# Third copy buffers, moved layernorm statistics, a later store in the output projection and an early exponential, in a fused attention and gated-MLP kernel

## Chip, core and metric

The kernel runs on one core of one Trainium2 chip. The metric is the device time of one execution in microseconds (us). The time before is the median of three runs. Engines are named as in the profile: PE (TensorE, matmuls and transposes; PEld is its weight load), DVE (VectorE), ACT (ScalarE), POOL (GpSimd), SP (SyncE, which issues the DMAs here; SPq is its queue).

## What is computed

```python
def _A_ref(x, wqkv, wo):                      # x: 1 x 2048 x 576
    H = 32; Dh = D // H; W = 256              # Dh = 18
    q, k, v = heads of x @ wqkv
    scores = q @ k.T * Dh ** -0.5
    mask = (i - j >= 0) & (i - j < W)
    p = softmax(where(mask, scores, -1e9))
    return (p @ v) @ wo

def _B_ref(x, w_in, w_sp, b_sp, w_out):       # w_in: 576 x 4608, w_sp: 2048 x 2048
    z = gelu(x @ w_in)
    z1 = z[..., :Fh];  z2 = layernorm(z[..., Fh:])
    g = w_sp @ z2 + b_sp                      # over the tokens
    return (z1 * g) @ w_out

xn = layernorm(x)
out = x + _A_ref(xn) * silu(_B_ref(xn))
```

## The kernel before

Every fp32 product is made of three products of rounded halves: a value's high part is rounded by ACT, its low part is the DVE's difference of the value and the high part (`split`, L115 and L116). PE therefore has most of the work. One execution goes through these stages, one after the other on PE.

**Stage 1, 0 to 57 us.** x comes in four chunks of 512 tokens. For each chunk DVE makes the layernorm statistics (`stats_of`, L303 and L304: four tiles with two BN_STATS and a BN_AGGR each), and a chain of one square root on ACT (L119) and seven small DVE instructions makes scale and shift (`scales_of`, L120 to L125 and L310). ACT normalizes (`norm_act`, L327), PE transposes eight 64-column blocks and then a ninth (`turn_group`, L337, PSUM tile `tpt`), and `form` splits the result: ACT the high part (L352), DVE the low part (L354). In between PE makes the first products for q and k, `narrow(j, c)` (L380): five column groups j of the weights for the 256 tokens of c, 54 matmuls each into a pair of PSUM banks, `ma` and `mb`. `keep_narrow` empties the pair into `qkhl`, ACT the high half (L115), DVE the low half (L116). All queues run in program order, so the place of `stats_of(2)` and `scales_of(2)` in the text is their place in DVE's queue.

**57 to 428.6 us.** The rest of q and k, v (copied out of PSUM at L909), and z2 with its Gelu on ACT (L946).

**Attention with z1 as filler, 428.6 to 894.4 us.** Sixteen units: eight groups of four heads for each half of the tokens. Each unit needs, in this order:

- *maxima*: matmuls `sp` (L598), whose row maximum DVE takes (L602, tile `mx`); `max_split` makes `ms` (L612); when all 32 are there, `max_end` transposes `ms` on PE (L621), DVE copies it (`mhl`, L624) and four DMAs write it as two extra rows into `att`, the tile that holds q (L628). These rows are what subtracts the maximum in the scores;
- *scores*: matmuls `tps` (L722), exponential on ACT (`pt`, L726), triangle masks on POOL (L734, L737);
- *pv*: products of `pt` with v into one PSUM bank `ops` (L750, one buffer), copied by ACT into `ou` (L765) when four blocks of rows are done;
- *the end of a unit* (`finish`): the sums of the exponentials are one row per head of `ou`; they go by DMA to `den`, are inverted by DVE (`invert`, L785), go to DRAM and come back spread over the partitions in `rp` (L792); POOL multiplies in four pieces (`divide`, L796) and four DMAs store the result (L801, o_d).

The maxima, the scores and the 1944 matmuls of z1 (`ma`, `mb`, L669, copied by ACT into `z1o` at L674 and stored at L571) each use half of PE's rows, so that two *lanes* run side by side; pv products and the transpose use all of its rows and both lanes stand still for them. The order is found while the program is built: a planner keeps a clock for each lane and for the busy time of the other engines, and in a loop takes whatever its rules allow: `pv_now` and `pv_run` for pv, `max_end` for full maxima, then the scores and maxima, and a fill matmul when nothing else is ready. A list `waiting` holds what is to be issued at a later reading of the planner's clock (loads, the steps of `finish` at `INVERT_AT`, `FETCH_AT` and `DIVIDE_AT`). The planner's clock decides the order alone; it is no time of the chip.

**wo, 894.4 to about 955 us.** Sixteen blocks n of 28 matmuls each (L1155) multiply the attention result by wo; `wo_load(t)` fetches what blocks 2t and 2t+1 need, `wo_split(t)` splits it (`ohl`, L1141 and L1142). The last unit is finished inside this loop: its sums are fetched at n == 1, divided and stored at n == 2. Each block's result is copied by ACT (`so`, L1188) and stored one block later (s_d, L1190).

**955 us to the end.** The product with w_sp (L1434), then with w_out (L1525), sum and store.

## Time and profile before

| | before |
|---|---|
| three runs | 1858.68, 1856.02, 1855.85 us |
| median | 1856.02 us |
| profiled execution | 1856.53 us, of which 1854.5 us are the span of the trace |
| attention stage | 465.8 us, of which PE is busy 452.22 us |
| wo stage, 894.4 to 955 us | 60.6 us, PE busy 60.18 us |
| TensorE clock over the execution | 0.995 of full speed |

The span goes from the first to the last instruction of the trace; 2.03 us of the profiled execution lie around it. Rows that group instructions read: line, engine, operation, output <- inputs, shapes, count, busy us, mean ns, and idle time of the engine just ahead of them, with what ended it. Rows of the timeline read: start, duration, engine, line, and in brackets the idle time before. A row of waits gives the engine and the line that waited, what it waited for, the total in us, how often, and the longest.

### The profile page before, as it was taken

Reading aid. Unit: us, or ns where it says so; the run is one execution under the profiler, and the core shown is the slowest. Engines: PE = TensorE matmul, PEld = TensorE weight load, DVE = VectorE, ACT = ScalarE, POOL = GpSimd, SP = SyncE. Lnnn points to the kernel's source line nnn. Section 1 sums busy time; section 2 is a strip of 40 time slices with the busy share of each in tenths; the row PEclk is TensorE's granted clock in tenths of the full one; section 3 lists DMA queues with packets and bytes.
Section 4 is the critical chain, followed back from the end, with each engine's and each line's share of the span. In section 5 each row is a group of like instructions: output and inputs, shape, how many; then the busy total and the mean of one; then the engine's idle time right before and its main releaser. Section 6 shows DMA issues by size and latency. Waiting matters only on the chain.

```text
span 1854.5 us, 38148 instructions
## 1 busy us (share of the span) xinstructions
PE 1821.4 (98%) x14357; PEld 1588.3 (86%) x14357; DVE 1138.4 (61%) x2283; ACT 948.4 (51%) x1756; POOL 432.0 (23%) x507
## 2 busy tenths in 40 slices
PE   8999999998999999999999999999999999999998
PEld 7999999997777777776898878888888888899998
DVE  6411333456776767771246787667976576767876
ACT  5533322224666567667467565465454544444443
POOL 3332333334455455555100000021200000000000
PEclk8999999999999999999999999999999999999999
DMA  8795688887566666755777677788777556797554
GB/s 265 189 231 172 226 278 284 288 261 215 144 185 173 194 180 178 195 161 147 232 259 247 220 242 244 262 281 296 257 259 246 181 194 210 222 263 217 160 160 134
DMA packets 266920, 405.75 MB, mean 219 GB/s; under 512 B 52336, under 2 KB 180592, under 8 KB 266608
## 3 DMA queue, kind: packets, MB, share of 16 engines
q1 hardware_dynamic: 266736, 403.32, 70.8%
q8 instruction: 113, 1.85, 0.4%
q14 instruction: 71, 0.58, 0.1%
HBM read 285.35 MB, written 117.09 MB: 217 GB/s over the span
## 4 chain that ended last, share of the span: by engine, by line
PE 84%; DVE 6%; DMA 5%; SPq 2%; ACT 2%; issue 2%; POOL 0%; DVEq 0%; ACTq 0%; POOLq 0%
PE acc L1434 35%; PE mb L206 12%; PE c L1525 8%; PE ma L669 6%; PE mb L669 5%; PE ops L750 4%; PE ma L206 4%; PE tps L722 3%; PE sp L598 2%; PE wops L1155 2%; SPq L363 1%; DMA xr<-in_x_dram 1%; PE ma L380 1%; DMA st_d<-qkhl 1%; DVE junk L602 1%
## 5 line engine op out<-in xcount | busy, mean ns | idle before, releaser
L1434 PE MATMUL acc<-spl,zh 128*128 128x512 f32 x1008 | 392.7, 390 | 1.3 <-DVE spl L116 1.2
L1434 PE MATMUL acc<-sph,zl 128*128 128x512 f32 x1008 | 392.2, 389 | 0.0
L1434 PE MATMUL acc<-sph,zh 128*128 128x512 f32 x1008 | 392.1, 389 | 0.0
L602 DVE CUSTOM_DVE_ANT_0 junk<-sp,band 128x384 bf16<-128x384 f32 (+1 forms) x512 | 275.8, 539 | 114.1 <-PE sp L598 32.7
L726 ACT ACTIVATE pt<-tps 128x384 f32<-128x384 f32 (+2 forms) x576 | 232.0, 442 | 121.1 <-PE tps L722 77.9
L116 DVE TENSOR_TENSOR spl<-spr,sph 128x1024 fp32r<-128x1024 f32 x168 | 209.7, 1248 | 38.7 <-ACT sph L115 37.8
L669 PE MATMUL mb<-b,z1wh 64*128 64x512 f32 x648 | 225.8, 401 | 2.2 <-ACT z1o L674 1.7
L669 PE MATMUL ma<-b,z1wh 64*128 64x512 f32 x648 | 225.0, 399 | 0.6 <-ACT zt L946 0.4
L1434 PEld LDWEIGHTS acc<-spl,zh 128*128 128x128 f32 x1008 | 189.2, 188 | 42.4 <-DVE spl L116 3.3
L1434 PEld LDWEIGHTS acc<-sph,zh 128*128 128x128 f32 x1008 | 189.2, 188 | 39.3
L1434 PEld LDWEIGHTS acc<-sph,zl 128*128 128x128 f32 x1008 | 189.2, 188 | 39.2
L115 ACT ACTIVATE zh<-b 128x384 fp32r<-128x384 f32 x168 | 87.6, 521 | 213.6 <-PE acc L1434 213.5
L115 ACT ACTIVATE sph<-spr 128x1024 fp32r<-128x1024 f32 x168 | 176.1, 1048 | 12.4 <-DMA spr<-sc_d 7.2
L722 PE MATMUL tps<-att 56*128 56x384 f32 (+1 forms) x576 | 177.6, 347 | 3.9 <-DMA att<-mhl 2.6
L116 DVE TENSOR_TENSOR zl<-b,zh 128x384 fp32r<-128x384 f32 x168 | 98.4, 586 | 124.1 <-ACT zh L115 121.6
L598 PE MATMUL sp<-att 54*128 54x384 f32 (+1 forms) x512 | 161.6, 350 | 1.6 <-DVE mx L602 1.4
L1525 PE MATMUL c<-b,o 128*128 128x288 f32 x1056 | 143.9, 295 | 1.5 <-DVE o L116 1.4
L1525 PEld LDWEIGHTS c<-b,o 128*128 128x128 f32 x1056 | 141.0, 188 | 2.4 <-DVE o L116 2.2
L947 DVE BATCH_NORM_STATS2 st<-zt 128x6 f32<-128x384 f32 x96 | 49.2, 547 | 131.4 <-ACT zt L946 131.3
L669 PE MATMUL ma<-b,z1wl 64*128 64x512 f32 x324 | 128.9, 398 | 0.0
L669 PE MATMUL mb<-b,z1wl 64*128 64x512 f32 x324 | 128.5, 397 | 0.0
L722 PEld LDWEIGHTS tps<-att 56*128 56x128 f32 x576 | 100.3, 185 | 32.6 <-issue 9.5
(220 smaller groups left out, 4187.6 us busy)
## 6 DMA issues: line engine op xcount, KB each, us to landing
spr<-sc_d SPq DMA_DIRECT2D x96, 512.0 KB
spr<-in_w_sp_dram SPq DMA_DIRECT2D x72, 512.0 KB
zr<-z_d SPq DMA_DIRECT2D x144, 192.0 KB
z_d<-zt SPq DMA_DIRECT2D x48, 384.0 KB
z_d<-z1o SPq DMA_DIRECT2D x72, 256.0 KB
z1t<-z_d SPq DMA_DIRECT2D x72, 256.0 KB
y_d<-z1t SPq DMA_DIRECT2D x72, 256.0 KB
a<-in_w_sp_dram SPq DMA_DIRECT2D x64, 256.0 KB
```

The lines of the kernel that those rows point to most:

```text
L115: act.activation(hi, src, AF.Copy)
L116: dve.tensor_tensor(lo, src, f32(hi), ALU.subtract)
L206: pe.matmul(banks[h][:, :n], *both[h][i], start=i == 0, stop=i == STEPS - 1)
L598: pe.matmul(ps[:, :w], q_of(u, j)[0:54, i * P:(i + 1) * P], k_of(u, j)[0:54, k0:k0 + w], start=True, stop=True)
L602: dve.tensor_tensor_reduce(out=junk[:, :w], in0=ps[:, :w], in1=band[:, m0:m0 + w], scale=1.0, scalar=-3.0e38, op0=ALU.add, op1=ALU.max, ac ...
L669: pe.matmul(ps, w, x_, start=n == 0, stop=n == STEPS - 1)
L722: pe.matmul(ps[:, :m * P], k_of(u, j)[:, (kb - base) * P:(kb - base + 1) * P], q_of(u, j)[:, (a - lo) * P:(a - lo + m) * P], start=True, s ...
L726: act.activation(pt[:, j, d0:d0 + n * P], ps[:, (qa - a) * P:(qa - a + n) * P], AF.Exp, scale=scale)
L750: pe.matmul(o_ps[c][32 * j:32 * j + 32, (qa - 4 * c) * P:(hi - 4 * c + 1) * P], vgs[u][:, kb - k0, j * VW:j * VW + 32], pt[:, j, (qa - kb) ...
L947: dve.bn_stats(st2[:, s, pc, :], zv)
L1434: pe.matmul(acc[j], z[:, ps], w[:, cs], start=s == i == 0 and n in OPENS, stop=s == 7 and i == 2, skip_group_check=True)
L1525: pe.matmul(banks[key][:, :288], y, w, start=begin and k == n == 0, stop=close and k == 8 and n == 2, skip_group_check=True)
```

## The change

- **Attention, buffers:** three `ou` tiles instead of two, two `rp` instead of one, three `z1o` instead of two. With them the steps of a unit's end come later: inversion, fetch and division have new planner times, and leftover parts are forced out three units behind instead of two (`part(u - 3)`), or when more than four are left two units behind.
- **Attention, planner:** pv is not begun while the copy out of the only `ops` bank is still under way (`ops_free`), and a run of pv products ends after a copy. The transpose of the maxima waits 1000 ns of the planner's clock after `ms`, and is taken on its own only when one of the next eight scores belongs to its unit. The first unit's scores are held 2500 ns longer. What is due is issued in the order of its due time.
- **Stage 1:** `stats_of(2)` moves from behind `keep_narrow(2, 0)` to behind `keep_narrow(4, 0)`, and `scales_of(2)` from ahead of `narrow(4, 0)` to behind `keep_narrow(0, 1)`.
- **Exponential:** one exponential of one column stands in the text ahead of the attention loop.
- **wo:** the last unit's sums are fetched after the store of block 0's result instead of before; the division stays at n == 2; its four stores move from n == 2 to n == 4, where the loads for t = 4 and t = 5 now both stand.

Every engine issues the same instructions as before, by kind and number, apart from the one exponential and one more table load on ACT.

```diff
-INVERT_AT = 6500
-FETCH_AT = 8500
-DIVIDE_AT = (20000, 21200, 22400, 23600, 26500, 27000, 27500, 28000)
+INVERT_AT = 11000
+FETCH_AT = 8000
+DIVIDE_AT = (28000, 29200, 30400, 31600, 37000, 38000, 39000, 40000)
+LATE = 1000
+DUE = 8
...
             keep_narrow(2, 0, banks)
-            stats_of(2, range(4))
             wq_high(4)
...
             form(*forms)
-            scales_of(2, range(4))
             banks = narrow(4, 0)
             form(turn_group(1, [8]))
             fetch(6, w_qk[6])
             keep_narrow(4, 0, banks)
+            stats_of(2, range(4))
             for j in range(5):
                 banks = narrow(j, 1)
...
                 keep_narrow(j, 1, banks)
                 done = None
+                if j == 0:
+                    scales_of(2, range(4))
                 if j < 2:
                     norm_act(2, (2 * j, 2 * j + 1))
                 if j == 0:
                     stats_of(3, range(4))
...
-                for w in list(waiting):
+                for w in sorted(waiting, key=lambda w: w[0]):
...
-                max_ready[u] = clock + wait + 400 + MAX_NS
+                max_ready[u] = clock + wait + 400 + MAX_NS + (2500 if u == 0 else 0)
...
-                                zo = zw.tile([P, 512], F32, name="z1o", bufs=2)
+                                zo = zw.tile([P, 512], F32, name="z1o", bufs=3)
...
+            ops_free = [0.0]
...
-                        while parts.get(u - 2):
-                            part(u - 2)
-                        ous[u] = (ap_.tile([P, HS], F32, name="ou", bufs=2) if u < NU - 1 else
+                        while parts.get(u - 3):
+                            part(u - 3)
+                        ous[u] = (ap_.tile([P, HS], F32, name="ou", bufs=3) if u < NU - 1 else
                                   tail()[:, 0:HS])
...
                     free_at = use("act", 500, 120)
+                    ops_free[0] = free_at
...
+                while len(parts.get(u - 2, ())) > 4:
+                    part(u - 2)
-                rp = ap_.tile([P, HS], F32, name="rp", bufs=1) if u < NU - 1 else f32(slots[4][:, 0:HS])
+                rp = ap_.tile([P, HS], F32, name="rp", bufs=2) if u < NU - 1 else f32(slots[4][:, 0:HS])
...
-                    after(max(INVERT_AT - sooner, 4500), invert)
+                    after(4500 if sooner else INVERT_AT, invert)
...
-                        after(ns - sooner + (3500 if sooner else 0), partial(part, u))
+                        after(ns - (14500 if sooner else 0), partial(part, u))
...
                 load_v(0)
+                warm = aa.tile([P, 1], F32, name="warm", bufs=1)
+                act.activation(warm, eps_t, AF.Exp)
...
+                def max_due(v):
+                    queue = score_queue[0]
+                    return not queue or queue[min(DUE, len(queue) - 1)][0] >= v
+
                 def pv_now():
+                    if not o_ps and ops_free[0] + GUARD > clock:
+                        return 0
...
-                    for v in [v for v in maxima if taken.get(v) == 2 * RMN and max_done[v] <= clock]:
+                    for v in [v for v in maxima if taken.get(v) == 2 * RMN and max_done[v] + LATE <= clock]:
...
                             later.clear()
                             break
+                        if not o_ps:
+                            break
...
-                    full = [v for v in maxima if taken.get(v) == 2 * RMN and max_done[v] + GUARD <= clock]
+                    full = [v for v in maxima if taken.get(v) == 2 * RMN and max_done[v] + LATE <= clock
+                            and max_due(v)]
...
                 if n == 0:
                     put_last()
-                if n == 1:
-                    sums()
                 if n == 2:
                     divide()
+                if n == 4:
                     store()
-                if n in (0, 2, 4, 6, 8):
+                    oraws.append(wo_load(4))
+                if n in (0, 4, 6, 8):
                     oraws.append(wo_load(3 + n // 2))
...
                 if stores:
                     sp.dma_start(*stores.pop())
+                if n == 1:
+                    sums()
                 stores.append((s_d[n * P:(n + 1) * P, :], so))
```

**DVE in stage 1.** Before, in DVE's queue behind `keep_narrow(2, 0)`; `st_533` are the statistics of chunk 2, the rows L354 are the low parts of chunk 1's transposes:

```order
L116 TENSOR_TENSOR qkhl<-mb,qkhl 128x256
L303 BN_STATS st_533<-xr 128x6 x2
L304 BN_AGGR st_534<-st_533 128x2
L303 BN_STATS st_533<-xr 128x6 x2
L304 BN_AGGR st_534<-st_533 128x2
L303 BN_STATS st_533<-xr 128x6 x2
L304 BN_AGGR st_534<-st_533 128x2
L303 BN_STATS st_533<-xr 128x6 x2
L304 BN_AGGR st_534<-st_533 128x2
L116 TENSOR_TENSOR qkhl<-ma,qkhl 128x256
L116 TENSOR_TENSOR qkhl<-mb,qkhl 128x256
L354 TENSOR_TENSOR b_95<-tpt,b_92 128x256
```

Now, further on in the same queue, from the last of chunk 2's statistics (`st_732`) to the first of chunk 3's (`st_826`); ahead of these rows the low parts L356 follow the two `qkhl` pairs directly:

```order
L305 BN_STATS st_732<-xr 128x6 x2
L306 BN_AGGR st_733<-st_732 128x2
L118 TENSOR_TENSOR qkhl<-ma,qkhl 128x256
L118 TENSOR_TENSOR qkhl<-mb,qkhl 128x256
L122 RECIPROCAL st_736<-st_734 128x4
L123 TENSOR_SCALAR st_735<-st_733 128x4
L124 TENSOR_TENSOR st_735<-st_735,st_736 128x4
L125 TENSOR_TENSOR st_735<-st_735,st_736 128x4
L126 TENSOR_SCALAR st_735<-st_735 128x4
L127 TENSOR_TENSOR st_736<-st_736,st_735 128x4
L312 SCALAR_TENSOR_TENSOR st_735<-st_733,st_736 128x4
L305 BN_STATS st_826<-xr 128x6 x2
```

The `qkhl` pair in the second list empties `narrow(0, 1)`. Behind it stand chunk 2's chain and all of chunk 3's statistics, and only then the pair that empties `narrow(1, 1)`; chunk 2's statistics stand right ahead of it instead of ahead of chunk 1's low parts.

**PE at a change of the `ops` bank.** Before, in a later unit of attention. The first row merges two pv products for four heads each: the last four matmuls of one bank's content and the first four of the next.

```order
L722 MATMUL tps<-att_2214 128x384
L669 MATMUL mb<-b_97,z1wh 128x512
L669 MATMUL ma<-b_97,z1wh 128x512
L722 MATMUL tps<-att_2213 128x384
L750 MATMUL ops<-pt,vg 32x128 x8
L750 MATMUL ops<-pt,vg 32x256 x4
L722 MATMUL tps<-att_2213 128x384
```

Now, at such a change in the same stage:

```order
L754 MATMUL ops<-pt,vg 32x256 x4
L754 MATMUL ops<-pt,vg 32x128 x4
L601 MATMUL sp<-att_2215 128x384
L726 MATMUL tps<-att_6835 128x256
L726 MATMUL tps<-att_6837 128x256
L601 MATMUL sp<-att_6833 128x384
L601 MATMUL sp<-att_2215 128x384
L672 MATMUL ma<-b_93,z1wh 128x512
L672 MATMUL mb<-b_96,z1wh 128x512
L672 MATMUL ma<-b_96,z1wh 128x512
L672 MATMUL mb<-b_93,z1wl 128x512
L754 MATMUL ops<-pt,vg 32x128 x4
```

Before, a row with `32x128 x8` stands at four places, and none is left; between the last product of one bank and the first of the next there are now always scores, maxima or fill matmuls.

**ACT around the exponentials.** Before, from the end of z2 to the first scores:

```order
L946 ACTIVATE zt<-mb 128x384
L119 ACT_TABLE_LOAD
L119 ACTIVATE sd_6816<-mv_84,eps_t 128x16
L674 ACTIVATE z1o<-mb 128x512
L674 ACTIVATE z1o<-ma 128x512
L684 ACTIVATE z1wh<-z1raw 128x384 x3
L726 ACT_TABLE_LOAD
L726 ACTIVATE pt<-tps 128x384 x7
```

Now, first where the new exponential stands (`qkhl` are the last of q and k, `ve` the copies of v), then at the first scores:

```order
L287 ACTIVATE wv1h<-wraw 128x9x96
L117 ACTIVATE qkhl<-ma 128x512
L117 ACTIVATE qkhl<-mb 128x512
L1016 ACT_TABLE_LOAD
L1016 ACTIVATE warm<-eps_t 128x1
L916 ACTIVATE ve<-ma 128x16x18
L916 ACTIVATE ve<-mb 128x16x18
```

```order
L953 ACTIVATE zt<-mb 128x384
L121 ACT_TABLE_LOAD
L121 ACTIVATE sd_6816<-mv_84,eps_t 128x16
L677 ACTIVATE z1o<-mb 128x512
L677 ACTIVATE z1o<-ma 128x512
L687 ACTIVATE z1wh<-z1raw 128x384 x3
L677 ACTIVATE z1o<-mb 128x512
L677 ACTIVATE z1o<-ma 128x512
L730 ACT_TABLE_LOAD
L730 ACTIVATE pt<-tps 128x384 x18
```

The new exponential, with a table load of its own, has gone ahead of the copies of v, far in front of z2's Gelu and the square root, and the load ahead of the first `pt` is still there.

6 lines of the change are left out of this document (3 added, 3 removed).

## The prediction

> **What bounds the kernel now.** I begin with the page: the busy shares, then the granted clock in 40 slices.
>
> ```profile
> span 1854.5 us, 38148 instructions
> PE 1821.4 (98%) x14357; PEld 1588.3 (86%) x14357; DVE 1138.4 (61%) x2283; ACT 948.4 (51%) x1756; POOL 432.0 (23%) x507
> PEclk8999999999999999999999999999999999999999
> ```
>
> PE is busy for 1821.4 of 1854.5 us, so 33.1 us of idle time is all that an order of work can win, and beside it what a halved clock costs. No instruction but one exponential and its table load is added or taken away, so every term below is a wait or a stretch at a lower clock. The second view is the busy time by stage (columns: PE, PEld, DVE, ACT, POOL, then clock, DMA share, GB/s).
>
> ```profile
> 0.00:57.00 57.00, 48.45 (x700) 46.61 (x702) 37.39 (x124) 33.08 (x68) 23.49 (x18) 0.91 0.80 258
> 428.60:894.40 465.80, 452.22 (x4425) 344.30 (x4426) 294.29 (x1043) 304.50 (x742) 243.11 (x355) 0.99 0.64 176
> 894.40:955.00 60.60, 60.18 (x450) 59.90 (x451) 16.11 (x19) 30.32 (x44) 3.53 (x2) 1.00 0.75 246
> ```
>
> The change touches these three stages. PE is idle for 8.55 us of the first, 13.58 us of attention and 0.42 us of wo. The third view says what PE waited for, over the whole span; the fourth groups PE's pv products, POOL's division and ACT's copy in attention.
>
> ```profile
> PE sp L621 <- DVE ms L612: 2.9, 5, 0.9
> PE tpt L337 <- DVE b L354: 2.9, 1, 2.9
> PE tps L722 <- DMA att<-mhl: 2.6, 1, 2.6
> PE mb L669 <- ACT z1o L674: 1.7, 4, 0.9
> PE wops L1155 <- DVE ohl L1142: 0.4, 1, 0.4
> ```
>
> ```profile
> L750 PE MATMUL ops<-pt,vg 128*32 128x128 f32 x448 | 23.5, 281 | 4.3 <-ACT ou L765 1.9 <-issue 1.7 <-POOL ou L796 0.8
> L796 POOL TENSOR_TENSOR ou<-ou,rp 128x256 f32<-128x256 f32 x60 | 43.6, 745 | 16.0 <-DMA rp<-r_d 14.1 <-DMA att<-st_d 1.9
> L765 ACT ACTIVATE ou<-ops 128x512 f32<-128x512 f32 x30 | 18.1, 604 | 10.9 <-PE ops L750 9.6 <-DMA o_d<-ou 1.2
> ```
>
> These are the waits that the parts of the change name: the transpose for `ms`, the low parts of stage 1, the first unit's rows, the fill for `z1o`, wo for `ohl`, and pv for the copy out of its bank.
>
> **The change part by part**, against the profiled execution of 1856.53 us (its span of 1854.5 and 2.03 around it; the runs' median, 1856.02, is 0.5 lower).
>
> *The first unit's scores.* The timeline shows the wait, and slices of 3.41 us show the clock around it (the column ahead of the last two is the clock).
>
> ```profile
> 444.30 0.45 PE L722 MATMUL tps<-att 56*128 56x384 f32 x2 [2.65 <-DMA att<-mhl]
> 441.90:445.30 3.40, 1.00 (x10) 1.00 (x11) 0.42 (x3) 0.78 (x2) 2.45 (x3) 1.00 0.56 152
> 445.30:448.72 3.42, 2.85 (x16) 2.14 (x14) 1.25 (x5) 2.62 (x5) 0.32 (x1) 0.51 0.86 251
> 448.72:452.13 3.41, 3.41 (x21) 3.12 (x18) 1.54 (x8) 1.69 (x4) 0.90 (x2) 0.50 0.70 169
> ```
>
> PE stood for 2.65 us, and in the two slices behind it 2.85 + 3.41 = 6.26 us of work ran at half clock, which is 3.1 us lost. Now the pace of a fill matmul in one lane, from the end of the stage:
>
> ```profile
> 893.00 0.40 PE L669 MATMUL ma<-b,z1wh 64*128 64x512 f32 x1
> 893.24 0.39 PE L669 MATMUL ma<-b,z1wl 64*128 64x512 f32 x1
> ```
>
> It is 0.24 us, and by width 0.18 us for 384 columns. Between unit 0's transpose and its first score there stood 42 fill and 10 maximum matmuls; by the order it is 60 and 13. Shared by two lanes that is 18 x 0.24 / 2 + 3 x 0.18 / 2 = 2.4 us more. So 0.25 us of the wait is left and the clock stays: **-5.5** (2.4 + 3.1). If the rows land 2 us later than before as well, nothing is won: bounds -5.7 and 0.
>
> *The ops bank.* 4.3 us of PE idle ahead of pv in the grouped row. All four merged `32x128 x8` rows are gone and other work stands there. At the fifth wait ACT's copy itself waited 1.2 us for the stores of an older `ou` (the L765 row), which the third buffer removes. I take four fifths, since the copy's 0.6 us is hidden only where enough matmuls follow: **-3.5** (bounds -4.3 and -1).
>
> *The transposes.* 2.9 us in five waits. They now come 1000 ns of the planner's clock later, or join a pv run; again four fifths: **-2.3** (bounds -2.9 and 0).
>
> *Third z1o.* The fill's waits of 1.7 us on ACT have one cause that a buffer can remove, this one:
>
> ```profile
> 644.61 0.60 ACT L674 ACTIVATE z1o<-mb 128x512 f32<-128x512 f32 x1 [0.96 <-DMA z_d<-z1o]
> ```
>
> **-1.0** (bounds -1.0 and 0).
>
> *The lanes.* The planner's new order also balances the lanes anew. Between two steps that need all of PE's rows, the stretch lasts as long as the longer lane. Counting each lane's matmuls in each stretch of the order and pricing them at 0.24 us for 512 columns and less by width, the longer lanes sum to 319 us before and 322 us now; 83 stretches with pv or a transpose behind them in both: **+2.7** (bounds 0, if a lane that is ahead only meets an engine later, and +2.7).
>
> *wo.* The 0.4 us wait for `ohl` has a visible chain.
>
> ```profile
> 914.74 0.65 ACT L1188 ACTIVATE so<-wops 128x576 f32<-128x576 f32 x1 [7.74 <-DMA s_d<-so]
> 902.96 3.53 POOL L796 TENSOR_TENSOR att<-att,att 128x512 f32<-128x512 f32 x2 [15.74 <-DMA att<-r_d]
> ```
>
> SP stood at the four stores until POOL's division ended at 906.5; the s_d stores behind it were late, so ACT stood for 7.74 us, and the next `ohl` with it. Behind the moved stores now stand the loads for t = 4 and 5, whose data block 8 needs; wo's 60.6 us hold 16 blocks, 3.8 us each, so from n == 4 there are 15 us, and the division has 7.6 us more before SP meets its stores: **-0.4** (bounds -0.4 and 0).
>
> *Statistics.* a row of ACT's and five of DVE's timeline in stage 1, and then PE by slices, the last three rows for the matmuls of `narrow` alone:
>
> ```profile
> 29.78 0.39 ACT L115 ACTIVATE qkhl<-mb 128x256 fp32r<-128x256 f32 x1
> 29.00 0.81 DVE L303 BATCH_NORM_STATS2 st<-xr 128x6 f32<-128x288 f32 x2
> 32.74 0.41 DVE L116 TENSOR_TENSOR qkhl<-ma,qkhl 128x256 fp32r<-128x256 f32 x1
> 33.41 3.38 DVE L354 TENSOR_TENSOR b<-tpt,b 128x256 fp32r<-128x256 f32 x8
> 36.70 0.17 DVE L120 RECIPROCAL st<-st 128x4 f32<-128x4 f32 x1
> 37.84 0.42 DVE L354 TENSOR_TENSOR b<-tpt,b 128x256 fp32r<-128x256 f32 x1
> ```
>
> ```profile
> 32.30:35.70 3.40, 1.44 (x23) 1.00 0.89 259
> 36.79:42.64 5.85, 5.84 (x54) 5.85 (x56) 0.51 1.00 300
> 42.64:45.71 3.07, 3.07 (x58) 3.07 (x56) 1.00 1.01 395
> 48.77:51.83 3.06, 3.06 (x58) 3.04 (x54) 1.00 0.61 139
> ```
>
> Before, the statistics held DVE from 29.00 to 32.74, 3.75 us, then came the low parts; PE's ninth transposes waited 2.9 us for them, the slice from 32.30 held 1.96 us of idle, and `narrow(0, 1)` ran at half clock, 5.85 instead of 3.07 us. Without the statistics DVE's `qkhl` pair follows ACT's, which ends at 30.17, and the low parts start at about 30.65, 2.75 us earlier; the wait goes, and PE starts `narrow(0, 1)` at 36.79 - 2.75 = 34.05 at full clock; after it `narrow(1, 1)` and `narrow(2, 1)` end at 43.25. But `narrow(3, 1)` needs the banks of `narrow(1, 1)`, and DVE comes to them late: low parts to 34.05, the ninth (0.42) and `qkhl(4, 0)` (0.75), with ACT's parts ahead of them, to 35.9, chunk 2's statistics to 39.65, `qkhl(0, 1)` at 0.75 to 40.4, the chain (36.70 to 37.84, 1.14) to 41.5, chunk 3's statistics to 45.25, `qkhl(1, 1)` to 46.0. So what is late next is DVE, and PE waits 2 to 2.7 us there, say 2.4, until 45.65. Before, `narrow(3, 1)` began at 48.77: 3.1 us won, if the clock stays up. Where PE stood for 2.40 of 3.40 us (441.90) and for 1.96 (32.30), the next slice was granted half. A wait of 2.4 us is as long, so I take one slice at half clock, 1.7 us: **-1.4** (bounds -3.1 at full clock and +0.3 with two slices at half).
>
> [...]
>
> *The early exponential.*
>
> ```profile
> 444.81 1.28 ACT L726 ACT_TABLE_LOAD   x1 [2.62 <-issue]
> 144.44 0.41 ACT L909 ACTIVATE ve<-ma 128x288 f32<-128x288 f32 x1 [1.33 <-POOL ve L908]
> ```
>
> It stands ahead of the copies of v now, where ACT was idle for 1.33 us waiting for POOL: that hides its load of 1.28 us. The load ahead of the first `pt` stays, so nothing is won: **0** (bounds -1.3 if the load at 444.81 were off the path after all, +1.3 if the new one is on it).
>
> *Sum*: -5.5 - 3.5 - 2.3 - 1.0 + 2.7 - 0.4 - 1.4 = -11.4, so 1856.53 - 11.4 = 1845.1, and 0.5 less against the median: **1844.6**. The best ends add up to -18.7, the worst to +3.3.
>
> **Rivals.**
>
> - *The clock falls in attention again.* The rows of unit 0 land as late after its first score as before, because the DMAs for `att` ahead of them moved too. Then the first term is 0 and the sum -5.9: 1850.1. For it: SP has the same loads ahead of the rows. Against: the score waits 2.4 us of matmuls longer.
> [...]
> - *It doesn't do what it says.* The planner's clock isn't the chip's; as old waits close, as many open at other transposes, copies and scores, and the ops, transpose and z1o terms (6.8) are 0, with the first term halved (2.75): -11.4 + 9.55 = -1.85, or 1854.2. For it: a planner's prices made the waits of before too. Against: the order has other work at each of the places.
> - *Slower: POOL's divisions in front of the masks.* They move from 20 to 28 us of the planner's clock after a unit's end to 28 to 40, into the next units' masks, and pv waits for a mask that stands behind one. A division takes 0.745 us, and there are 60 (the L796 row). At 15 of them fully on the path the 11.4 us are gone; at 30, half of them, it is 1845 + 22 = 1867. For it: 0.8 us of pv's idle is already put down to L796. Against: POOL is busy 243 of 466 us, and its 14.1 us of standing for `rp` in front of masks go with a second `rp`.
>
> **How the numbers follow.** My forecast gets 0.57, the clock in attention 0.20, the other rule 0.05, the waits that come back 0.12, the divisions 0.06. This kernel's measurement can tell about 0.2%, 3.7 us: under 1852.3 is faster, over 1859.7 slower. The first three cases are faster (0.82), the fourth is the same (0.12), the last slower (0.06). The range for 8 in 10 goes from the best end, 1838, to 1852, which takes in the first three cases.
>
> **What would show it.** In the profile after: no row of PE `tps` waiting for `att<-mhl` above 1 us and the clock slices around 445 at 1.00; L750's idle under 1 us; the transposes' row under 1 us; in stage 1 the 2.9 us at L337 gone, a new wait of 2 to 2.7 us on `qkhl` near 43 to 46, and half clock for one slice behind it; wo's `ohl` row gone; a table load near 143 us and one at the first `pt`. Wrong would be: attention longer than 460 us, a wait of pv for POOL's masks or of a score for its rows in later units, or a stage 1 that ends no earlier than 56.

## The result, and the profile after

Both kernels ran 22 times. The median fell from 1856.16 us to 1849.88 us (1846.38 to 1855.74); the ratio is 0.9966, with a 95% interval of 0.9958 to 0.9973. That is 6.3 us, or 0.34%, faster: inside the stated range of 1838 to 1852, a little over half of the 11.4 us that the sum gave. The profiled execution took 1852.91 us, with a span of 1851.2; it lies 3 us above its median, while that of before (1856.53) lay 0.4 us above its own. So the two traces show only 3.3 of the 6.3 us, and the runs below, which repeat most of this order, have to serve for the rest. Of all runs in this document one, of the statistics alone below, fell in a slow state (2083.76 us at a clock of 0.88); its ratio leaves it out, and without it the median given there would be 1852.22.

The page of the changed kernel:

```profile
span 1851.2 us, 38133 instructions
PE 1824.6 (99%) x14357; PEld 1582.7 (85%) x14357; DVE 1137.1 (61%) x2283; ACT 948.2 (51%) x1758; POOL 430.7 (23%) x507
```

PE's idle time fell from 33.1 to 26.6 us, but its busy time grew by 3.2. Of that 2.2 us lie in attention, where one more slice of 3.41 us than before ran at half clock. By stage (PE, PEld, DVE, ACT, POOL, clock, DMA share, GB/s):

```profile
0.00:57.00 57.00, 51.26 (x720) 48.34 (x722) 39.12 (x127) 35.80 (x73) 25.38 (x19) 0.97 0.79 261
427.00:891.20 464.20, 454.42 (x4424) 349.75 (x4424) 293.67 (x1041) 303.05 (x741) 242.23 (x355) 0.99 0.69 176
891.20:951.50 60.30, 59.94 (x451) 59.52 (x450) 15.28 (x20) 29.93 (x45) 2.54 (x2) 1.00 0.77 251
```

Attention took 465.8 us before and takes 464.2, wo 60.6 and 60.3. What PE waited for, over the whole span, and its two groups that were counted on in attention:

```profile
PE tps L726 <- ACT pt L730: 5.4, 5, 3.6
PE ma L382 <- DVE qkhl L118: 2.5, 2, 1.7
PE ma L672 <- ACT z1o L677: 2.4, 1, 2.4
PE wops L1173 <- DVE ohl L1160: 0.4, 1, 0.4
```

```profile
L754 PE MATMUL ops<-pt,vg 128*32 128x128 f32 x448 | 23.3, 280 | 0.0
L624 PE MATMUL sp<-ident,ms 128*64 128x128 f32 x16 | 4.8, 299 | 0.4 <-DVE mx L605 0.3
```

The waits of pv (4.3 us) and, but for 0.3 us, of the transposes (2.9 us) are gone, as is the one at L337. But attention is longer than 460 us, which the prediction had named as a sign of being wrong. Three other waits stand in their place, and each is a row of its own in the timeline. **At the first scores**, PE's rows, then ACT's:

```profile
447.06 0.49 PE L672 MATMUL ma<-b,z1wh 64*128 64x512 f32 x1 [2.35 <-ACT z1o L677]
448.86 0.69 PE L726 MATMUL tps<-att 56*128 56x384 f32 x1 [1.08 <-ACT pt L730]
```

```profile
440.36 1.36 ACT L687 ACTIVATE z1wh<-z1raw 128x384 fp32r<-128x384 f32 x3 [4.29 <-DMA z1raw<-in_w_z_dram]
443.10 0.60 ACT L677 ACTIVATE z1o<-mb 128x512 f32<-128x512 f32 x1 [1.38 <-PE sp L601]
446.41 0.60 ACT L677 ACTIVATE z1o<-ma 128x512 f32<-128x512 f32 x1 [2.71 <-DMA z_d<-z1o]
447.03 1.28 ACT L730 ACT_TABLE_LOAD   x1
```

The scores' rows came in time: no wait for `att<-mhl` is left. But the 18 more fill matmuls complete a second block of z1 on both lanes, so a third and a fourth `z1o` copy now stand ahead of the first exponential in ACT's queue. The fourth needs the first one's tile, whose store SP issued only at 442.91, after the four `att<-mhl` that held SP from 434.99 to 441.63 and three more copies into `att`. The copy waited 2.71 us, the table load and the exponentials came behind it, and PE stood for 2.35 and 1.08 us, as long as the 2.65 and 0.57 of before. The clock fell behind it as well (PE busy, then the clock):

```profile
443.60:447.00 3.40, 1.01 (x5) 1.00 0.78 209
447.00:450.40 3.40, 2.26 (x11) 0.67 0.66 205
450.40:453.80 3.40, 3.40 (x20) 0.50 0.87 239
```

**At 670 us** there is a wait that before did not have, shown by PE's row and ACT's:

```profile
670.08 0.69 PE L726 MATMUL tps<-att 56*128 56x384 f32 x1 [3.58 <-ACT pt L730]
```

```profile
669.24 0.52 ACT L687 ACTIVATE z1wh<-z1raw 128x384 fp32r<-128x384 f32 x1 [4.33 <-DMA z1raw<-in_w_z_dram]
```

SP's row for that load, and PE by a slice behind the wait:

```profile
662.09 0.36 SPq L641 DMA_DIRECT2D z1raw<-in_w_z_dram  x1
```

```profile
669.99:673.40 3.41, 3.32 (x17) 0.50 0.90 201
```

The load was issued at 662.09 and had landed 7.1 us later, but ACT was ready for it after 2.8 us (669.24 less 4.33 is 664.91). Such a load stands in the program where the later of the two lanes begins with the set of weights before it (54 matmuls in each lane), and the split of what it loads where the earlier lane is half through that set. Here the lanes began 3.1 us apart (654.4 and 657.5), and SP came to the load 4.5 us after the later one, with the `att<-mhl` rows of a unit, copies into `att` and a store ahead of it. Which of the two weighs more was not tried. The exponentials stand behind the split of z1's weights, and the scores behind the exponentials; behind the wait a slice ran at half clock.

**In stage 1** the wait at L337 is gone and one for DVE's `qkhl` is there; PE's row, and PE by slices:

```profile
44.56 0.38 PE L382 MATMUL ma<-b,wqh 64*128 64x256 f32 x1 [1.66 <-DVE qkhl L118]
```

```profile
41.90:45.31 3.41, 1.75 (x24) 1.00 0.86 340
45.31:48.72 3.41, 3.41 (x36) 0.51 0.55 134
```

From the first transposes of chunk 1 to the first wide product of q and k it took 29.16 to 56.48, 27.32 us, and now

```profile
28.38 1.15 PE L339 MATMUL tpt<-ident,xpair 64*128 64x64 f32 x30
54.24 0.48 PE L208 MATMUL ma<-b,wqh 64*128 64x512 f32 x1
```

25.86 us: 1.46 us less, with one slice at half clock. (The 0.78 us by which the first row is early lie ahead of the change.)

### The profile page after: what moved, and what is told of

Read it like the earlier page. It is cut to its first block, busy times and chain, and to the rows that moved or that the text cites. A ratio compares the mean times of both kernels' runs of the same rounds, so it can differ in the third digit from the quotient of the medians.

```text
span 1851.2 us, 38133 instructions
## 1 busy us (share of the span) xinstructions
PE 1824.6 (99%) x14357; PEld 1582.7 (85%) x14357; DVE 1137.1 (61%) x2283; ACT 948.2 (51%) x1758; POOL 430.7 (23%) x507
## 4 chain that ended last, share of the span: by engine, by line
PE 83%; DVE 6%; DMA 5%; SPq 2%; ACT 2%; issue 2%; POOL 0%; DVEq 0%; ACTq 0%; POOLq 0%
PE acc L1454 34%; PE mb L208 11%; PE c L1545 8%; PE ma L672 6%; PE mb L672 5%; PE ma L208 5%; PE ops L754 5%; PE tps L726 3%; PE sp L601 2%; PE wops L1173 2%; SPq L365 1%; DMA z1raw<-in_w_z_dram 1%; DMA xr<-in_x_dram 1%; PE mb L382 1%; DMA att<-st_d 1%
```

## The experiments

One measure serves for attention in most of them: from the first fill matmul of z1 to the start of the last wo matmul, so that it doesn't matter how the order mixes the two stages. It is 525.9 us before (428.68 to 954.6) and 524.3 after (427.04 to 951.3). Each ratio is to runs of the kernel before taken beside those of the experiment, and is not exactly the quotient of the two medians.

**Four z1o tiles.** The edit to the changed kernel:

```diff
-                                zo = zw.tile([P, 512], F32, name="z1o", bufs=3)
+                                zo = zw.tile([P, 512], F32, name="z1o", bufs=4)
```

> The changed kernel with four z1o tiles instead of three; the order on every engine is the same. Theory A: in the changed kernel the first exponentials stood behind a fourth z1o copy on ACT, which waited 2.71 us for the store of the first one, because 18 more fill matmuls ahead of the first score complete another block of z1 on both lanes. With a fourth tile the copy runs at once: PE's wait of 2.35 us for z1o near 447 us goes, the wait of 1.08 us for the first exponentials stays or moves forward by 2 us, the clock behind it stays at 1.00, and the time is 3 to 6 us under the changed kernel (ratio to before about 0.994). Theory B (the rows of the maxima, or the z1 weights, are late themselves): PE waits for att<-mhl or for z1wh at the same place, the clock still falls, and the time is within 1 us of the changed kernel (0.9966).

Measured: 1846.86 us, ratio 0.9955 (0.9944 to 0.9967), and 516.7 us from fill to wo, 7.6 less. ACT's rows, and PE by slices:

```profile
443.99 0.59 ACT L677 ACTIVATE z1o<-ma 128x512 f32<-128x512 f32 x1
444.60 1.28 ACT L730 ACT_TABLE_LOAD   x1
```

```profile
443.60:447.00 3.40, 2.21 (x17) 1.00 0.81 259
447.00:450.40 3.40, 3.40 (x36) 1.00 0.79 195
```

The copy runs at once, the table load is 2.4 us earlier, PE's wait for it is gone (1.07 us for the exponentials stays) and no slice here is halved. By the trace theory A holds: the tile that came third was one too few for the order that came with it. The time agrees less clearly: it is 3.0 us under the changed kernel by the medians and 2.0 by the ratios, whose intervals touch, where 3 to 6 us were expected. With three tiles the wait also differs from execution to execution: 2.35 and 2.07 us in the changed kernel, and 0.90 and 0.41 in two of the next kernels, whose order in attention is the same. The clock fell at this place in all four; from fill to wo half clock cost them 4.7, 4.6, 4.7 and 3.2 us.

**No hold on the first unit.**

```diff
-                max_ready[u] = clock + wait + 400 + MAX_NS + (2500 if u == 0 else 0)
+                max_ready[u] = clock + wait + 400 + MAX_NS
```

> The changed kernel without the 2500 ns by which the first unit's scores are held back; the planner then orders the whole of attention anew. Theory A (the hold swapped one wait for another): the wait of PE for att<-mhl of about 2.6 us comes back at the first score, the fourth z1o copy no longer stands ahead of the first exponentials, the clock falls as in both kernels, and the time is within 1.5 us of the changed kernel (ratio to before 0.996 to 0.9975). Theory B (the hold is worth what the prediction gave it, 5.5 us): 3 us or more above the changed kernel, ratio to before 0.998 to 1.0.

Measured: 1848.92 us, ratio 0.9969 (0.9957 to 0.9981), 519.5 us from fill to wo. The larger waits of PE in attention:

```profile
441.16 0.45 PE L726 MATMUL tps<-att 56*128 56x384 f32 x2 [0.63 <-DMA att<-mhl]
443.51 0.44 PE L726 MATMUL tps<-att 56*128 56x384 f32 x1 [0.98 <-ACT pt L730]
584.38 0.44 PE L726 MATMUL tps<-att 56*128 56x384 f32 x1 [1.60 <-ACT pt L730]
612.17 0.45 PE L726 MATMUL tps<-att 56*128 56x384 f32 x1 [3.30 <-ACT pt L730]
```

The hold isn't worth 5.5 us; without it the time is the same. But theory A was wrong in its picture: the wait for `att<-mhl` came back at 0.63 us only, and the clock didn't fall (idle time and half clock around the first scores come to 2.2 us, as against 6.9 in the changed kernel), so the hold wasn't needed beside the rest of the change. The late z1 weights are there too, at two other places (584.38 and 612.17).

**Statistics back.** The statistics and scales of chunk 2 at their places of before, the rest as changed.

```diff
             keep_narrow(2, 0, banks)
+            stats_of(2, range(4))
...
             form(*forms)
+            scales_of(2, range(4))
...
             keep_narrow(4, 0, banks)
-            stats_of(2, range(4))
...
-                if j == 0:
-                    scales_of(2, range(4))
```

> The changed kernel with the layernorm statistics and scales of chunk 2 back where they were before; attention's order is that of the changed kernel. The theory of the prediction: the wait of 2.9 us at the ninth transposes and two slices at half clock come back, the wait of 2 us for the banks of narrow(1, 1) goes, and the first stage is about 1 us longer than in the changed kernel (ratio to before about 0.9972). The rival (the move is worth 3 us, the rest of attention less): ratio 0.998 or more. Beside it: if the wait of 3.6 us at 670 us in the one profile of the changed kernel belongs to the order, it is here too, since nothing from 60 us on has changed; if it was a slow load of one execution, it is not.

Measured: 1851.87 us, ratio 0.998 (0.9971 to 0.999). PE's waits in stage 1 and at 667 us:

```profile
35.83 0.34 PE L339 MATMUL tpt<-ident,xpair 64*128 64x64 f32 x4 [2.85 <-DVE b L356]
666.78 0.44 PE L725 MATMUL tps<-att 56*128 56x384 f32 x1 [2.94 <-ACT pt L729]
```

The wait at the ninth transposes is back at 2.85 us, and the same stretch of stage 1 takes 26.1 us (28.41 to 54.52), only 0.2 us more than in the changed kernel, with one slice at half clock here and not the two that were expected (the clock is 0.94 over the first 57 us, before it was 0.91). And the wait near 667 us is here too: it belongs to the order. By the two ratios the move is worth 0.0014, 2.6 us. The ratio is the one from which the rival was to hold, but the interval takes in the 0.9972 of the other theory too, so it decides for neither.

**Statistics of chunk 3 later.**

```diff
-                if j == 0:
-                    stats_of(3, range(4))
                 if j == 1:
+                    stats_of(3, range(4))
+                if j == 2:
                     done = scales_of(3, range(4))
```

> The changed kernel with the statistics of chunk 3 behind keep_narrow(1, 1) instead of behind keep_narrow(0, 1), and its scales behind keep_narrow(2, 1). If DVE's queue is what held narrow(3, 1) for 2 us and halved the clock behind it, both go: the first stage is 2.5 to 3.7 us shorter than in the changed kernel, ratio to before about 0.995. If something else held it (ACT's normalization, or the transposes of chunk 2), the wait stays or comes back within 10 us and the ratio is 0.996 to 0.997. A wait of 3.6 us at 670 us, as in the changed kernel's profile, is here too only if it belongs to the order.

Measured: 1852.95 us, ratio 0.9983 (0.9972 to 0.9993), on the same chip as the three above. PE's waits:

```profile
44.47 0.38 PE L382 MATMUL ma<-b,wqh 64*128 64x256 f32 x1 [1.00 <-DVE qkhl L118]
54.37 0.34 PE L339 MATMUL tpt<-ident,xpair 64*128 64x64 f32 x4 [1.83 <-DVE b L356]
```

The rival holds for the waits. With DVE free, 1.00 us of the wait stays, because ACT's part of `qkhl(1, 1)` (43.59) stands behind the normalization that waits for chunk 2's chain; and the statistics, put off, delay chunk 2's low parts, where PE loses 1.83 us ten microseconds later, with a slice at half clock behind it (a wide matmul takes 0.39 us up to 55.31 and 0.63 us from 55.82 on). The ratio is above the 0.996 to 0.997 that the rival allowed; what makes it so is not shown.

**The changed kernel again,** with no edit.

> The changed kernel once more, beside the next three on one chip. Both theories: ratio to before 0.9958 to 0.9973 as measured. In its profile the theory that the wait of PE for the exponentials near 664 to 670 us belongs to the order expects it again, at 2 to 4 us, with ACT's z1wh waiting for the load of z1raw just ahead; the theory of a chance event expects none above 1 us.

Measured: 1850.59 us, ratio 0.9974 (0.9959 to 0.9989); 524.4 us from fill to wo.

```profile
668.79 0.69 PE L726 MATMUL tps<-att 56*128 56x384 f32 x1 [3.19 <-ACT pt L730]
```

In five executions of this order (the first profile, four z1o, statistics back, statistics late, and this one) the wait was 3.58, 2.25, 2.94, 2.58 and 3.19 us. It is no chance event. In each of the five a slice or two at half clock followed; with four z1o tiles, where nothing else from fill to wo ran at half clock, it cost 1.7 us.

**z1's weights a block earlier.** A second `z1raw` tile, and the load for f + 2 issued when the second half of f begins; only SP's queue changes:

```diff
+                                if b == 1 and n == 0 and f + 2 < FH // P and f + 2 not in raws and f + 2 not in z1w:
+                                    load_raw(f + 2)
```

> The changed kernel with two z1raw tiles, the load of z1's next weights issued one block of z1 (27 fill matmuls) earlier; only SP's queue changes, the orders of PE, ACT and DVE are those of the changed kernel. Theory A: the wait near 664 to 670 us is ACT's z1wh, which stands in front of the exponentials and waits for a load issued only 7 us before. With the earlier load it goes (PE below 0.5 us there), and so does ACT's wait for z1raw at 440 us; the time is 2 to 4 us under the changed kernel of the same call. Theory B: ACT is late there for another reason (the scores come late because the transposes of the maxima were put off), PE still waits 2 us or more near 665 us, and the time is within 1 us.

Measured: 1847.99 us, ratio 0.9952 (0.9934 to 0.997), 2.6 us under the changed kernel that ran beside it (their intervals overlap), and 519.6 us from fill to wo. No wait of PE above 0.2 us near 665 us is left, so theory A holds there; ACT's wait for z1raw near 440 us, which it expected to go as well, is still 2.6 us. At the first scores it was worse; PE's row and ACT's:

```profile
447.32 0.79 PE L679 MATMUL ma<-b,z1wh 64*128 64x512 f32 x1 [3.60 <-ACT z1o L684]
```

```profile
446.67 0.60 ACT L684 ACTIVATE z1o<-ma 128x512 f32<-128x512 f32 x1 [3.96 <-DMA z_d<-z1o]
```

One more load stands in SP's queue ahead of the store that the fourth `z1o` waits for. SP issued that store at 441.13 and the copy could begin 5.5 us later; in the changed kernel that took 3.5 us (442.91 to 446.41). So it was not issued late but took longer; that the added load's data made it so is likely, but was not tried.

**Transposes by the old rule.**

```diff
-                    for v in [v for v in maxima if taken.get(v) == 2 * RMN and max_done[v] + LATE <= clock]:
+                    for v in [v for v in maxima if taken.get(v) == 2 * RMN and max_done[v] <= clock]:
...
-                    full = [v for v in maxima if taken.get(v) == 2 * RMN and max_done[v] + LATE <= clock
-                            and max_due(v)]
+                    full = [v for v in maxima if taken.get(v) == 2 * RMN and max_done[v] + GUARD <= clock]
```

> The changed kernel with the transposes of the maxima by the old rule (as soon as they are full by the planner's clock, not 1000 ns later and not by need); the planner orders attention anew. The prediction's term: the waits of the transposes for DVE come back, 2.3 to 2.9 us in about five pieces, and the time is 2 to 3 us above the changed kernel of the same call. The rival (putting the transposes off packs fill matmuls together and so makes the late z1 weights): the wait for the exponentials near 665 us goes as well, and the time is within 1 us of the changed kernel or below it.

Measured: 1867.72 us, ratio 1.0062 (1.004 to 1.0084), 539.0 us from fill to wo: 17 us slower than with the rule, and slower than before. PE's waits, and ACT's in attention:

```profile
PE tps L726 <- ACT pt L730: 13.7, 7, 4.7
PE sp L624 <- DVE ms L615: 0.9, 1, 0.9
```

```profile
ACT z1wh L687 <- DMA z1raw<-in_w_z_dram: 24.1, 8, 5.8
```

Both expectations fell. Of the transposes' waits only one came back, 0.9 us, and putting transposes off is not what makes the weights late: without it, ACT waits for z1's weights in eight places, and in five of them PE stands for 1.6 us or more. What the trace shows is that the lanes drift apart in this order: six of the eight loads stand at sets of weights that the later lane begins 7.1 to 9.3 us after the earlier (4.8 us at most in the kernel before, 5.6 in the changed kernel), and the lead of the load shrinks by that distance. Of the 14.6 us more from fill to wo, 7.4 are idle time of PE, 3.1 the clock, and 4 us PE's work at whole clock. Why this order lets the lanes drift, and what makes the 4 us, was not tried.

**All mended.** Four `z1o` tiles, the earlier loads, and:

```diff
                 rsqrt_of(rstd2, mv2[:, :, 1], sd2, tm2)
+                warm = aa.tile([P, 1], F32, name="warm", bufs=1)
+                act.activation(warm, sd2[:, 0:1], AF.Exp)
...
-                warm = aa.tile([P, 1], F32, name="warm", bufs=1)
-                act.activation(warm, eps_t, AF.Exp)
...
             keep_narrow(2, 0, banks)
+            stats_of(2, range(2))
...
             keep_narrow(4, 0, banks)
-            stats_of(2, range(4))
+            stats_of(2, range(2, 4))
...
-                if j == 0:
-                    stats_of(3, range(4))
-                if j == 1:
+                if j < 2:
+                    stats_of(3, range(2 * j, 2 * j + 2))
+                if j == 2:
                     done = scales_of(3, range(4))
```

> The changed kernel with four z1o tiles, z1's weights loaded one block earlier, the exponential's table loaded right behind the square root of z2, and the statistics of chunks 2 and 3 in halves between the qkhl pairs. If the four causes named so far are the causes: no wait of PE above 1 us from 30 us to the end of attention, no slice at half clock behind 20 us, attention about 456 to 458 us, and 8 to 11 us under the changed kernel of the same call (ratio to before 0.991 to 0.993). If the waits only move on: within 4 us of the changed kernel, with new waits of 1 us and more.

Measured: 1842.71 us, ratio 0.9926 (0.9908 to 0.9945), 7.9 us under the changed kernel that ran beside it. Attention by the view of stages, and its longest wait:

```profile
428.00:881.00 453.00, 449.20 (x4425) 346.26 (x4426) 294.33 (x1041) 302.83 (x742) 242.26 (x355) 1.00 0.69 181
```

```profile
447.56 0.35 PE L602 MATMUL sp<-att 54*128 54x256 f32 x1 [1.19 <-DMA att<-st_d]
```

Attention takes 453.0 us, 11.2 less than in the changed kernel's profile; PE is idle for 3.8 us of it, the clock is whole, and no wait for an exponential or for `z1o` above 0.3 us is left. The exponential that depends on the square root's result brings the table at 430.49, 14.6 us ahead of the first `pt` (445.07). In stage 1 two waits of 0.99 and 2.15 us stay, but no slice from 20 us on is at half clock (0.999 over the execution). So the causes named so far are the main ones. Two waits, 1.19 and 2.15 us, are longer than the 1 us that was expected as the most, and the gain is at the lower end of what was expected.

**The ops rule alone,** put into the kernel before:

```diff
+            ops_free = [0.0]
...
+                    ops_free[0] = free_at
...
+                    if not o_ps and ops_free[0] + GUARD > clock:
+                        return 0
...
+                        if not o_ps:
+                            break
```

> The kernel before with one part of the change alone: pv is not begun while the copy out of the ops bank is under way, and a run of pv ends after a copy. The prediction's term: the 4.3 us that PE waits ahead of pv fall below 1 us, everything else stays, and the time falls by 3 to 4 us (ratio 0.998). The rival, from the runs so far (a new order shifts z1's fill against its loads and copies): the pv waits go, but the wait of the first unit's scores stays and a wait for the exponentials of 2 us or more appears; ratio 0.999 to 1.002.

Measured: 1864.3 us, ratio 1.0052 (1.0032 to 1.0071): slower, which neither expectation had. The profiled execution was the longest of six, 1871.09 us. PE's waits, and a row of DVE's timeline:

```profile
PE sp L598 <- DVE mx L602: 7.5, 6, 3.5
PE ops L751 <- ACT ou L766: 2.0, 1, 2.0
```

```profile
765.30 0.35 DVE L787 RECIPROCAL den<-den 128x32 f32<-128x32 f32 x1 [4.40 <-DMA den<-ou]
```

The pv waits go, except one: the copy out of the bank stood 2.16 us for the store of an old `ou`, which a third tile would remove (not tried alone). But the new order puts DVE's inversion of `den` ahead of row maxima while its load is still under way, SP having issued it at 761.01; the maxima behind it wait, PE waits for them (3.46 us at 766.13), and the clock falls there (0.91 over 760 to 800 us) and, behind other waits, in two more stretches (0.87 over 444 to 470 and 0.98 over 800 to 899 us). In the changed kernel the inversions wait for `den` 0.6 us in all; their later place, 11000 instead of 6500 ns of the planner's clock, would explain why the rule does no harm there, but the old times beside the rest of the change were not tried. In the changed kernel itself the rule is idle: with its lines taken out, the program comes out the same, instruction by instruction.

**Statistics alone,** put into the kernel before:

```diff
             keep_narrow(2, 0, banks)
-            stats_of(2, range(4))
...
-            scales_of(2, range(4))
...
             keep_narrow(4, 0, banks)
+            stats_of(2, range(4))
...
+                if j == 0:
+                    scales_of(2, range(4))
```

> The kernel before with the moved statistics alone; from 60 us on every order is that of before. The prediction's term: the wait of 2.9 us at the ninth transposes goes, one of 2 to 2.7 us for qkhl appears with one slice at half clock behind it, and the time falls by 1.4 us (between 3.1 us and nothing; ratio 0.9983 to 1.0). The rival, from the undone move (2.6 us apart by the two medians, but on two chips): 2.5 us or more, ratio 0.9987 or less. A reading of the first trace pair says 0, ratio 1.0.

Measured: 1852.88 us, ratio 0.9985 (0.9971 to 0.9999). PE by slices around the new wait, and the first wide product:

```profile
43.00:45.30 2.30, 0.66 (x12) 1.00 1.02 403
45.30:48.70 3.40, 3.40 (x56) 1.00 0.55 129
```

```profile
53.27 0.47 PE L206 MATMUL ma<-b,wqh 64*128 64x512 f32 x1
```

From the first transposes at 29.03 that is 24.24 us, 3.1 less than before: the same wait of 1.64 us, and this time no slice at half clock. So both values that the prediction wrote down occur, -1.4 with a fallen clock and -3.1 without. The interval of the ratio takes in both; the reading of 0 lies just outside it.

**Repairs without the change.** The repairs of the kernel with all mended, put into the kernel before; PE's order is that of before. The edit is that of the kernel with all mended, on the lines of before, with

```diff
-                                zo = zw.tile([P, 512], F32, name="z1o", bufs=2)
+                                zo = zw.tile([P, 512], F32, name="z1o", bufs=4)
```

> The kernel before with the four repairs of the run before last (four z1o tiles, z1's weights loaded a block earlier, the exponential's table behind the square root, statistics in halves) and none of the planner's changes; PE's order is that of before. Theory A (the planner's changes are worth what they removed, about 7 us of ops, transpose and z1o waits): those waits stay, and the time is 5 to 8 us above the kernel with all repairs and the changes: ratio to before 0.996 to 0.997. Theory B (the repairs carry the gain, the planner's order adds nothing): ratio 0.993.

Measured: 1853.36 us, ratio 0.9987 (0.9975 to 1.0); 523.2 us from fill to wo. PE's waits:

```profile
PE sp L623 <- DVE ms L614: 3.5, 6, 0.9
PE ops L761 <- issue: 1.7, 2, 0.9
PE ops L761 <- ACT ou L776: 1.4, 2, 0.9
```

The waits that the planner's changes remove are all here, and from fill to wo it takes 10.1 us more than with both. Theory A holds, and by more than it asked: the ratio lies above its 0.996 to 0.997. The change alone took 0.0034 off the time (0.0026 when it ran again), the repairs alone 0.0013, and both 0.0074, by these values more than the two added up.

**All mended, statistics whole.** The kernel with all mended, with

```diff
-            stats_of(2, range(2))
...
-            stats_of(2, range(2, 4))
+            stats_of(2, range(4))
...
-                if j < 2:
-                    stats_of(3, range(2 * j, 2 * j + 2))
-                if j == 2:
+                if j == 0:
+                    stats_of(3, range(4))
+                if j == 1:
                     done = scales_of(3, range(4))
```

> The kernel with the repairs and the change, but the statistics as the change has them, whole and not in halves. If halves are what lifted the clock in stage 1: the wait of 1.7 us for qkhl and a slice at half clock are back, first stage 1.5 to 2.5 us longer, ratio to before 0.9935 to 0.994. If the halves only moved a wait (1.0 and 2.2 us at transposes were seen with them): within 1 us of it, ratio 0.9925 to 0.993.

Measured: 1841.97 us, ratio 0.9935 (0.9917 to 0.9954); 513.5 us from fill to wo.

```profile
44.13 0.38 PE L382 MATMUL ma<-b,wqh 64*128 64x256 f32 x1 [1.64 <-DVE qkhl L118]
52.19 0.48 PE L208 MATMUL ma<-b,wqh 64*128 64x512 f32 x1
```

The wait for `qkhl` is back, but the clock stayed up (1.00 in every microsecond from 41 to 54), and the stretch took 24.24 us (27.95 to 52.19), as against 25.08 with halves. The ratio alone would speak for halves, but the interval takes in both expectations, and the longer stage and the half clock that were to make it are not in the trace; halves bring nothing that was shown.

## Why the prediction was right in sign, and what was mis-sized

- **The first unit's scores, -5.5: this step failed.** It said that 0.25 us of the wait is left and the clock stays. The rows were indeed in time. But the 18 matmuls that delay the scores were taken as time only, and they carry work for another engine: each 27 end in a copy on ACT, and the new copies stand ahead of the exponentials. The wait moved from `att<-mhl` to `z1o` at the same length, the clock fell, and the term was about 0 in the profile: PE's idle time around the first scores and what half clock cost there come to 6.6 us before and 6.9 after. In three more executions of the order they are 5.2, 5.0 and 4.0 us, without the hold 2.2, and with four z1o tiles 1.6, which is 5.0 under the profile before. So the tile shows the cause. The price of before isn't fixed either: with the statistics alone, in the same order, the clock stayed up there and it is 3.4. The rival that the clock falls again had 1850.1, for another reason than it gave; that the 1849.9 meet it is luck, since it too lacks the late weights and has the lanes too high.
- **Ops bank, -3.5, and transposes, -2.3:** the waits went, by 4.3 and 2.6 us. But they aren't gains of the parts that were made for them. The ops rule alone is 7.8 us slower by the medians and does nothing in the changed kernel, and without the transposes' rule hardly any of their waits come back. What removes them is the order as a whole; which part of it, the third `ou` or the later inversion, was not tried singly.
- **Third z1o, -1.0:** the wait of 0.9 us near 645 us is gone.
- **The late z1 weights were missing from the sum:** 2.3 to 3.6 us of waiting in all five executions, and 4.0 to 6.2 with the half clock behind it. Apart from attention's first load, for which ACT waits in both kernels, the shortest lead of such a load over its use is 7.3 us in the kernel before (615.59 to 622.88), and ACT did not wait; here it would have been 2.8. The prediction did not check how a new order changes the lead of loads that the change doesn't touch.
- **Lanes, +2.7:** mis-sized. A longer lane would show as PE's busy time at whole clock; by the table below that is the same in both orders.
- **Statistics, -1.4:** -1.46 in the profile, with one halved slice as forecast, and -3.1 where the clock stayed up; with the old place in the changed kernel the stretch was only 0.2 us longer, since one slice was halved there and not two. The wait itself was 1.66 us, under the 2 to 2.7 expected, since DVE reached `qkhl(1, 1)` sooner. No run shows the other rule of the clock, which had 0.05: behind this wait the clock was 0.51 in the slice from 45.31.
- **wo, -0.4:** the wait at 917.87 is gone, but one of 0.36 us stands at 937.04, so 0.
- **Early exponential, 0:** right; the load ahead of the first `pt` stood at 447.03. Placed behind the square root it hides whole, and the 1.07 us of PE goes.
- **POOL's divisions, the slower rival:** PE's longest wait for a mask ahead of pv is 0.2 us, of a weight load. It fell.

The stretch from fill to wo divides into PE's idle time, what half clock cost (half of PE's busy time in the halved slices), and the rest, PE's work at whole clock:

| execution | from fill to wo | idle | half clock | rest |
|---|---|---|---|---|
| before | 525.9 | 13.9 | 3.1 | 508.9 |
| statistics alone (order of before) | 524.4 | 14.5 | 0.0 | 509.9 |
| changed kernel | 524.3 | 10.1 | 4.7 | 509.5 |
| the changed kernel again | 524.4 | 10.0 | 4.6 | 509.9 |
| statistics back | 521.0 | 7.0 | 4.7 | 509.3 |
| statistics of chunk 3 later | 521.4 | 8.5 | 3.2 | 509.7 |
| four z1o tiles | 516.7 | 5.8 | 1.7 | 509.1 |
| all mended | 513.1 | 4.2 | 0.0 | 508.9 |
| transposes by the old rule | 539.0 | 17.4 | 7.7 | 513.9 |
| the ops rule alone | 539.5 | 16.9 | 9.4 | 513.2 |

The rest is 509 to 510 us in both orders, so the lanes cost nothing that can be seen; only the last two orders have 4 us more of it. In the two traces the sum is then +0.3 for the first scores, -4.3, -2.6 and -0.9 for the waits that went, +3.6 for the weights and +1.7 for the half clock behind them, +0.6 for the rest and -1.5 for the statistics: -3.1, and the traces differ by 3.3 us. The medians' 6.3 holds another 3 us that these two traces don't show; executions of this order differ by as much (521.0 to 524.4 us from fill to wo), in idle time and clock alone.

## What to carry to other kernels

When a hold is filled with other work, follow that work through to the engines that finish it: its copies, stores and loads join queues in front of the very thing that was held. A part of this planner's change had no price of its own; a wait that it removes is worth its length only if the loads and copies on the other engines keep their lead in the new order, so check the shortest lead of each, from its issue to the moment its user is ready, before and after. And undo parts both ways, from the changed kernel and from the one before: the ops rule was idle in one and harmful in the other.

## What the runs showed of the hardware

The clock fell behind shorter gaps than the 1.96 and 2.40 us on which the prediction rested. Behind the one gap of 1.63 to 1.67 us in stage 1, a slice at half clock followed in five executions (the changed kernel twice, four z1o, no hold, earlier loads) and none in three (transposes by the old rule, statistics alone, all mended with statistics whole): in the microsecond from 47 to 48 the clock is 0.50 in all five, and in every one from 41 to 54 it is 1.00 in all three. What sets the three apart was not shown.

A table load cost its own 1.28 us and no more. In the kernel with all mended and statistics whole the square root ahead of it ends at 427.47, the load starts at 427.49, and the exponential behind it at 428.78.
